# All scores of the first batch computed in the first steps, ten steps of them kept in DRAM

## The chip, the cores and the metric

The kernel runs on one core of a Trainium2 chip. A core has TensorE (PE) for matmuls, with weight loads on a lane of their own (PEld), VectorE (DVE), ScalarE (ACT), GpSimd (POOL) and SyncE (SP), which here only issues DMAs. Each engine takes its instructions in program order; they wait for each other by semaphores. The metric is the time of one execution on the device in microseconds (us), lower is better.

## What is computed

```python
def _attn_ref(q, k, v):
    B, H, S, D = q.shape                      # 8, 8, 576, 64
    scores = np.matmul(q, k.transpose(0, 1, 3, 2)) / np.sqrt(D)
    kth = np.partition(scores, -32, axis=-1)[..., -32:-31]
    scores = np.where(scores >= kth, scores, -1e9)
    scores = scores - np.max(scores, axis=-1, keepdims=True)
    attn = np.exp(scores)
    attn = attn / (np.sum(attn, axis=-1, keepdims=True) + 1e-09)
    return np.matmul(attn, v)
...
h = x @ w_in                                  # x: 4608 x 512, w_in: 512 x 2048
g = np.where(h > 0, h, np.exp(np.minimum(h, 0)) - 1)
out = g @ w_out                               # 2048 x 512
```

Attention in which every query keeps its 32 highest scores, and behind it a feed-forward block with elu. x is the attention's output with the heads side by side. The weights arrive as 64-bit floats, and the kernel decodes them to 32 bits itself.

## The kernel before

**Steps.** The attention is cut into 144 steps, 18 for each of the 8 batches. A step is one tile of 128 queries for one pair of heads (hp 0 to 3). A batch has 4 full query tiles times 4 pairs, 16 steps, and 2 steps for its last 64 queries, each of which takes two pairs at once. In batch 0 steps 0 to 3 are tile 0 with pairs 0 to 3, steps 4 to 7 tile 1, and so on; steps 16 and 17 are the remainder. A main loop runs over n, and in turn n several steps are in work: the scores of n+2 (and n+3), the search for the top 32 of step n on DVE, mask, exp, transposition and product with V of the steps before.

**Of one step.** `transpose_qk` (line 259) turns keys and queries of a pair into a tile kq of 128 x 2 x 576 numbers: PE transposes to PSUM (266, 274) and ACT copies (271, 279). `scores` (292) does a step in two halves: matmuls to a PSUM tile (309), and ACT copies it to the tile sc (329). A full step has 8 matmul records, a remainder step 20. `first_max` (331) and `next_max` (338) on DVE find the 8 highest four times over and strike them out in between (334, 340, 346): 14 instructions of 0.74 us each, which is 9.64 us a step. `biases` and `mask` on POOL (351 to 359), `exp` on ACT (367), `trans` on PE (407, 425) with two ACT copies to et (412, 426), `attend` on PE (440). When a query tile has all its pairs, `sums` (374) inverts the sums of exp by way of a small DRAM tile (382, 394) and `normalise` on POOL (455) ends a tile xT, the input of the feed-forward block.

**Feed-forward pieces** (475 to 511) are small bundles of PE work. `feed` (527) deals them out to the turns by a plan of shares and due times: it counts pieces and turns and knows no times.

**Weights.** In the steps 0 to 6 (EARLY is 6) the weights are decoded beside the attention, one at each `weight_slot` (201): ACT splits a weight into two parts (183, 184), two slots later DVE joins them (189, 190) and POOL adds (194). The slots stand between the DVE instructions of a step, four in a step up to step 3 and six from step 4 on. Raw weights lie in buffers that become free with POOL's add; SP issues the next read (173) behind that.

**Keys.** In the first steps the four pairs of batch 0 are turned on the chip, two before the loop, one each in turns 0 and 1. `keep_kq` (281) writes each kq to DRAM (283), and `load_kq` (285) brings it back for later steps (289). Steps 0 to 3 use the tile on the chip; each later step of a batch reads its pair again, a remainder step two pairs. For batch 0 that is 4 writes and 16 reads of 576 KB. The scores of steps 2 to 7 are computed in turns 0 to 5, those from step 8 on in turns 6, 8, 10 and so on, two steps at a time.

**Buffers.** kq has 5, sc 5 and two spare tiles that are raw weight buffers at first, PSUM tiles for scores and transposes (ps_x) 2. The pool xT has 2: at first they take inputs of `load_qk` (214) for the pairs (0,1) and (0,2) and later (1,1), (1,2) and (2,0), then the feed-forward inputs. SP has 8 semaphores for its DMAs and uses them in turn, so a DMA goes out only when the eighth before it has landed.

The order of each engine is the order in which the program is written (`manual_schedule`); nothing is moved by a scheduler.

Of the kernel before, what the change touches and what calls it, by code (L numbers as in the profile page):

```python
# [10 lines left out]
FP32 = mybir.dt.float32  # L11
# [24 lines left out]
class Step:  # L36
# [5 lines left out]
    def __init__(self, n, g, hp, last):  # L42
        self.n = n
        self.g = g
        self.hps = (hp, hp + 1) if g.rem else (hp,)
        self.ends = self.hps[-1] == last
        self.turned = self.attended = self.summed = False


# [12 lines left out]
def kernel(  # L62
# [9 lines left out]
    nc = tc.nc  # L72
# [7 lines left out]
    NHP = H // 2  # L80
# [47 lines left out]
    def spare_tile(i, name):  # L128

        size = ((2 * J + 2) * P, 2 * S, 2 * WN)[i // 2]  # L130
        return spare.tile([P, size], FP32, tag=f"s{i}", name=name)
# [126 lines left out]

    def transpose_qk(b, hp):

        t = kqT[b, hp] = kqpool.tile([P, 2, S], FP32, tag="kq", name="kq")
        src = [loaded.pop((b, hp, name)) for name in "kq"]
        ps = ps_x.tile([P, 2, JP], FP32, tag="x", name="qkps")
        for n in range(2):
            for c in range(J):
                nc.tensor.transpose(  # L266
                    ps[:, n, c * P : (c + 1) * P],
                    src[n][:, c, :, :].rearrange("p h d -> p (h d)"),
                    ident[:],
                )  # L270
        nc.scalar.copy(t[:, :, 0:JP], ps[:])  # L271
        ps = ps_x.tile([P, 2, JP], FP32, tag="x", name="qkps")
        for n in range(2):
            nc.tensor.transpose(
                ps[:, n, 0:R],
                src[n][0:R, J, :, :].rearrange("p h d -> p (h d)"),
                ident[0:R, 0:R],
            )
        nc.scalar.copy(t[:, :, JP:S], ps[:, :, 0:R])

    def keep_kq(b, hp):
        kept[b, hp] = dram.tile([P, 2, S], FP32, tag=f"kq{b}{hp}", name="kqd")
        nc.sync.dma_start(kept[b, hp][:], kqT[b, hp][:])
# [5 lines left out]
            nc.sync.dma_start(u.kq[hp][:], kept[u.g.b, hp][:])  # L289


    def scores(u, half):
        g = u.g
        q0 = g.qt * P
        if half == 0:
            i = (u.n + 2) % 7 if u.n >= 10 else 0
            if i < 5:
                u.sc = scpool.tile([P, 2, S], FP32, tag="sc", name="sc")
            else:
                u.sc = spare_tile(i - 3, "sc").rearrange(  # L300
                    "p (i s) -> p i s", i=2
                )
        ks = slice(half * HS, (half + 1) * HS)

        ps = ps_x.tile([P, 2, JP], FP32, tag="x", name="scps")

        def product(j, hp, i, rows, at, keys):
            r = slice(i * D, (i + 1) * D)
            nc.tensor.matmul(  # L309
                ps[rows, j, at : at + keys.stop - keys.start],  # L310
                u.kq[hp][r, 1, q0 : q0 + g.ql],
                u.kq[hp][r, 0, keys],
                start=True,
                stop=True,
            )

        if g.rem:
            for i in range(2):
                k0 = half * HS + i * R
                n = min(HS, S - k0)  # L320
                for j, hp in enumerate(u.hps):
                    product(j, hp, i, (lo, hi)[i ^ j], 0, slice(k0, k0 + n))
                if n < HS:
                    for j, hp in enumerate(u.hps):
                        product(j, hp, i, (lo, hi)[i ^ j], n, slice(0, HS - n))
        else:
            for i in range(2):
                product(i, u.hps[0], i, slice(0, P), 0, ks)
        nc.scalar.copy(u.sc[:, :, ks], ps[:, :, 0:HS])  # L329
# [258 lines left out]
    def decode(n, place):  # L588

        if place in ((3, 4, 5, 6) if n < NHP else (0, 2, 3, 4, 5, 6)):  # L590
            weight_slot()
# [3 lines left out]
    def at(step, fn, *args):  # L595
        todo.setdefault(step, []).append((fn, args))
# [5 lines left out]
    for p, pair in enumerate(pairs):  # L602
        if p >= NHP:
            n = next((n for n in extra if p in extra[n]), None)
            if n is None:
                n = EARLY + 1 + 2 * (p - 10)
                turns[n] = pair
            at(n + 1, keep_kq, *pair)
        elif p >= 2:
            at(p - 1, keep_kq, *pair)  # L610
    for n, u in enumerate(steps[NHP:]):
        at(n + 1 if n + NHP < EARLY + 2 else (n + NHP) // 2 * 2 - 3, load_kq, u)
    for hp in range(1, NHP):
        at(hp, load_v, 0, hp)
    for b in range(1, B):
# [3 lines left out]
    with tc.manual_schedule():  # L619
        for hp in range(3):  # L620
            load_qk(0, hp)
        load_weights(3)
        for hp in range(2):
            transpose_qk(0, hp)
            steps[hp].kq = {hp: kqT[0, hp]}
            for half in range(2):
                scores(steps[hp], half)
            if hp == 0:
                load_qk(0, 3)
        load_weights()  # L630
        load_v(0, 0)
        first_max(steps[0])
        weight_slot()
        weight_slot()
        for hp in range(2):
            keep_kq(0, hp)
        for n in range(NS + 4):
            early = n < EARLY
            now, last, done = (
                steps[n + d] if 0 <= n + d < NS else None for d in (0, -1, -2)  # L640
            )
            for fn, args in todo.pop(n, []):
                fn(*args)
            gone = None
            if early:
                ahead = steps[n + 2]
                if n + 2 < NHP:
                    transpose_qk(0, n + 2)
                    ahead.kq = {n + 2: kqT[0, n + 2]}
                for half in range(2):  # L650
                    scores(ahead, half)
            elif n % 2 == 0:

                for d in (2, 3):
                    if n + d < NS:
                        for half in range(2):
                            scores(steps[n + d], half)
                    if d == 2:
                        for u in steps[n - 4 : n - 2]:
                            if not u.attended:  # L660
                                attend(u)
                                gone = u
            if n in turns:
                transpose_qk(*turns[n])
            if n >= EARLY and n + 2 in turns:
                load_qk(*turns[n + 2])
            if now and n > 0:
                first_max(now)
            if last:
                biases(last)  # L670
                mask(last, 0)
            if early:
                if last:
                    mask(last, 1)
                decode(n, 0)
                feed(n, 0.5)
                if last:
                    exp(last, 0)
                    exp(last, 1)
                next_max(now, (n, 1))  # L680
                decode(n, 2)
                if last:
                    trans(last)
                feed(n, 0.5)
                next_max(now, (n, 3))
                decode(n, 4)
                if last and last.ends:
                    load_weights(margin=0)
                    sums(last)
                if last:  # L690
                    attend(last)
                next_max(now, (n, 5))
                decode(n, 6)
                if last and last.ends:
                    normalise(last.g)
                for p in extra.get(n, []):
                    transpose_qk(*pairs[p])
                for p in fetch.get(n, []):
                    load_qk(*pairs[p])
                continue  # L700
            decode(n, 0)
            feed(n, (0.3, 0.7)[n % 2])
            if now:
                next_max(now, (n, 1))
            decode(n, 2)
            if last:
                mask(last, 1)
                exp(last, 0)
            if done and not done.turned:
                trans(done)  # L710
            if now:
                next_max(now, (n, 3))
            decode(n, 4)
            if gone and gone.ends:
                normalise(gone.g)
            feed(n, (0.3, 0.7)[n % 2])
            if now:
                next_max(now, (n, 5))
            decode(n, 6)
            if last:  # L720
                exp(last, 1)
            if done and done.ends and not done.summed:
                sums(done)
        while ffn:
            ffn.pop(0)[1]()
# [33 lines left out]
```

## Time and profile before

| | |
|---|---|
| time, median of 3 runs | 1669.07 us (1668.19 to 1669.85) |
| the profiled execution | 1668.57 us, its span 1666.8 us |
| PE busy | 1574.8 us (94%) |
| PEld busy | 1049.1 us (63%) |
| DVE busy | 1461.8 us (88%) |
| ACT busy | 918.2 us (55%) |
| POOL busy | 1154.1 us (69%) |
| granted PE clock, mean | 0.970 |
| DMA | 176.86 MB, mean 106 GB/s |

The profile is of one execution. A row of a timeline gives start, length, engine, line, operation, the tile written and the tiles read, their shapes, and in brackets the engine's idle time before and what ended it. A row of waits gives the total, the times and the longest. A busy share is a mean over stages of different kind: the first 136 us hold seven steps with weight decoding, then steps follow each other at 9.6 to 10.2 us, and after step 143 (1521 us) only feed-forward work is left. Matmul ends are modelled, so a busy PE is not PE at its peak.

### The profile page before, as it was taken

How to read it: one execution, taken by the hardware profiler on the slowest of the kernel's cores; microseconds unless marked ns; L12 is line 12 of the kernel's file. 1: busy time of each engine (PE TensorE's matmuls, PEld its weight loads, DVE VectorE, ACT ScalarE, POOL GpSimd, SP SyncE). 2: the span in 40 equal slices, each digit the busy share in tenths (PEclk: the TensorE clock that was granted, in tenths of full speed). 3: DMA queues.
4: the chain of work that ended last, by engine and by line, in shares of the span. 5: the costliest groups of instructions: out<-in, count | busy, mean ns of one | idle time of the engine just before them, and what ended most of it. 6: DMA issues, size and time to landing. Idle time of an engine off the chain costs nothing.

```text
span 1666.8 us, 28300 instructions
## 1 busy us (share of the span) xinstructions
PE 1574.8 (94%) x9792; PEld 1049.1 (63%) x9792; DVE 1461.8 (88%) x3065; ACT 918.2 (55%) x1877; POOL 1154.1 (69%) x1462
## 2 busy tenths in 40 slices
PE   5559899999999999998999999999999999999999
PEld 3346777777776675857566566566556566566565
DVE  6989999999999999999999989979989989987000
ACT  5566566566656564646466466456466466355121
POOL 4777777777778786878778678668668668668021
PEclk7569999999999999999999999999999999999999
DMA  9873555445363513121212321221212312210000
GB/s 329 227 242 124 162 163 147 148 145 154 111 198 96 190 39 117 64 84 70 85 71 100 112 88 61 77 84 64 91 70 100 112 60 89 77 42 8 26 7 13
DMA packets 139552, 176.86 MB, mean 106 GB/s; under 512 B 94352, under 2 KB 102544, under 8 KB 139408
## 3 DMA queue, kind: packets, MB, share of 16 engines
q1 hardware_dynamic: 135856, 174.16, 32.5%
q8 instruction: 78, 1.28, 0.3%
q10 hardware_dynamic: 3552, 0.89, 0.3%
q14 instruction: 66, 0.54, 0.1%
HBM read 146.54 MB, written 28.46 MB: 105 GB/s over the span
## 4 chain that ended last, share of the span: by engine, by line
PE 61%; DVE 24%; POOL 5%; issue 4%; ACT 4%; DMA 2%; SPq 1%; ACTq 0%; POOLq 0%; DVEq 0%
PE ops L499 21%; PE hps L475 20%; DVE m L346 11%; DVE wk L340 10%; PE scps L309 7%; PE avps L440 6%; PE eps L407 5%; DVE m L334 2%; POOL sc L359 1%; PE qkps L266 1%; POOL wk L357 1%; POOL wk L358 1%; POOL gT L492 1%; ACT sc L367 1%; DMA qin<-in_q_dram 1%
## 5 line engine op out<-in xcount | busy, mean ns | idle before, releaser
L346 DVE MAX8 m<-wk 128x8 f32<-128x576 f32 x864 | 609.5, 747 | 0.0
L475 PE MATMUL hps<-xT,w_in 128*128 128x128 f32 (+2 forms) x2432 | 531.7, 373 | 10.9 <-ACT gT L490 5.7
L499 PE MATMUL ops<-w_out,gT 128*128 128x512 f32 x1152 | 520.0, 597 | 7.1 <-ACT osb L508 7.1
L475 PEld LDWEIGHTS hps<-xT,w_in 128*128 128x128 f32 x2432 | 381.5, 192 | 136.1 <-issue 18.8
L359 POOL TENSOR_TENSOR sc<-sc,wk 128x576 f32<-128x576 f32 x288 | 407.1, 1414 | 23.9
L340 DVE MATCH_REPLACE8 wk<-m,wk 128x576 f32<-128x576 f32 x576 | 423.4, 743 | 0.0
L499 PEld LDWEIGHTS ops<-w_out,gT 128*128 128x128 f32 x1152 | 209.6, 190 | 240.3 <-issue 214.3
L367 ACT ACTIVATE sc<-sc,neg 128x576 f32<-128x576 f32 x288 | 224.1, 778 | 226.5 <-POOL sc L359 226.3
L492 POOL TENSOR_TENSOR gT<-gT,n 128x384 f32<-128x384 f32 (+1 forms) x168 | 187.3, 1121 | 192.3 <-ACT n L491 189.4
L357 POOL TENSOR_SCALAR wk<-sc,nth 128x576 f32<-128x576 f32 x288 | 215.5, 748 | 28.0
L329 ACT COPY sc<-scps 128x576 f32<-128x576 f32 x288 | 170.2, 639 | 89.9 <-PE scps L309 87.7
L309 PE MATMUL scps<-kq 64*128 64x288 f32 (+3 forms) x1344 | 187.7, 430 | 29.8 <-ACT kq L271 17.8
L340 DVE MATCH_REPLACE8 wk<-m,sc 128x576 f32<-128x576 f32 x288 | 211.7, 743 | 0.0
L334 DVE MAX8 m<-sc 128x8 f32<-128x576 f32 x288 | 201.2, 740 | 11.1 <-ACT sc L329 11.0
L358 POOL TENSOR_SCALAR wk<-wk 128x576 f32<-128x576 f32 x288 | 192.2, 667 | 23.8
L412 ACT COPY et<-eps 128x1024 f32<-128x1024 f32 x144 | 144.6, 1004 | 98.3 <-PE eps L407 97.3
L440 PE MATMUL avps<-et,vE 128*64 128x128 f32 (+1 forms) x3200 | 180.2, 269 | 6.1 <-ACT et L412 3.8
L440 PEld LDWEIGHTS avps<-et,vE 128*64 128x64 f32 x3200 | 162.0, 139 | 33.8 <-issue 25.1
L407 PEld LDWEIGHTS eps<-ident,sc 128*128 128x128 f32 x1152 | 135.7, 143 | 72.8 <-issue 36.6
L407 PE MATMUL eps<-ident,sc 128*128 128x128 f32 x1152 | 154.6, 277 | 21.8 <-ACT sc L367 19.7
L309 PEld LDWEIGHTS scps<-kq 64*128 64x128 f32 (+1 forms) x1344 | 104.9, 180 | 101.2 <-issue 39.5
L489 ACT ACTIVATE n<-hps 128x384 f32<-128x384 f32 (+1 forms) x168 | 90.1, 536 | 115.7 <-PE hps L475 107.3
(60 smaller groups left out, 910.0 us busy)
## 6 DMA issues: line engine op xcount, KB each, us to landing
kq<-kqd SPq DMA_DIRECT2D x156, 576.0 KB
kqd<-kq SPq DMA_DIRECT2D x32, 576.0 KB
rb<-recd SPq DMA_DIRECT2D x64, 128.0 KB
out_dram<-osb SPq DMA_DIRECT2D x32, 256.0 KB
kin<-in_k_dram SPq DMA_DIRECT2D x27, 256.0 KB
qin<-in_q_dram SPq DMA_DIRECT2D x26, 256.0 KB
raw<-in_moe_w_out_dram SPq DMA_DIRECT2D x12, 512.0 KB
vE<-in_v_dram SPq DMA_DIRECT2D x32, 128.0 KB
```

Of the source, the lines that this page charges most:

```text
L309: nc.tensor.matmul(ps[rows, j, at : at + keys.stop - keys.start], u.kq[hp][r, 1, q0 : q0 + g.ql], u.kq[hp][r, 0, keys], start=True, stop=True,
L334: nc.vector.max(u.m1[:, i, :], u.sc[:, i, :])
L340: nc.vector.match_replace(u.wk[:, i, :], u.m[:, i, :], u.cur[:, i, :], TAKEN)
L346: nc.vector.max(u.m[:, i, :], u.cur[:, i, :])
L357: nc.gpsimd.tensor_scalar(pen, s, u.nth[:, i : i + 1], 2.0**100, ALU.add, ALU.mult)
L358: nc.gpsimd.tensor_scalar(pen, pen, 0.0, TAKEN, ALU.min, ALU.max)
L359: nc.gpsimd.tensor_tensor(s, s, pen, ALU.add)
L367: nc.scalar.activation(s, s, AF.Exp, bias=u.neg[:, i : i + 1], scale=scale, accum_out=g.den[:, at : at + 1],)
L407: nc.tensor.transpose(ps[:, i, c * P : (c + 1) * P], e[:, k0 + c * P : k0 + (c + 1) * P], ident[:],)
L440: nc.tensor.matmul(g.av[r, hp, 0:ql], vE[g.b, hp][:, i, (c + i) % (J + 1), :], u.et[:, at, q0 : q0 + ql], start=(c == 0), stop=(c == J),)
L475: nc.tensor.matmul(ps[:, f % G, :], w_in[:, i, f * P : (f + 1) * P], blk.xT[:, i, 0:N], start=(i == 0), stop=(i == NC - 1),)
L499: nc.tensor.matmul(blk.o[:], blk.gT[f // NG][:, f % NG, s * P : (s + 1) * P], w_out[:, f, :], start=(f == 0), stop=(f == NF - 1),)
```

## The change

In batch 0 the keys are no longer written to DRAM and read back. The scores of all 18 steps are computed in turns 0 to 4 from the kq tiles on the chip (the line with `g.b > 0` in the diff). Those of steps 2 to 7 go directly to their sc tiles, as before, except that steps 6 and 7 are both done in turn 4. Those of steps 8 to 17 go through `scores_ahead`: ACT copies them to a tile of the pool xT (two buffers), SP writes this to DRAM, and `load_scores` reads it to the sc tile in turns 6, 8, 10, 12 and 14, where the scores were computed before. Where in a turn: steps 8, 9 at the end of turn 0; 10, 11 in turn 1 ahead of the exps, 12, 13 at its end; 14, 15 and 16, 17 the same in turn 2. A write is issued behind the next score of its kind or at the end of the turn. DVE's and POOL's instructions and their order are the same before and after; so are the feed-forward pieces.

```diff
+    def score_tile(u):
+        i = (u.n + 2) % 7 if u.n >= 10 else 0
+        if i < 5:
+            u.sc = scpool.tile([P, 2, S], FP32, tag="sc", name="sc")
+        else:
+            u.sc = spare_tile(i - 3, "sc").rearrange("p (i s) -> p i s", i=2)
+
+    waiting = []
+
+    def store_scores():
+        while waiting:
+            u, t = waiting.pop(0)
+            nc.sync.dma_start(u.scd[:], t)
+
+    def scores_ahead(u):
+        t = xtpool.tile([P, NC, T], FP32, tag="xT", name="scin")
+        t = t[:].rearrange("p c n -> p (c n)")[:, 0 : 2 * S]
+        u.sc = t.rearrange("p (i s) -> p i s", i=2)
+        for half in range(2):
+            scores(u, half)
+        u.scd = dram.tile([P, 2, S], FP32, tag=f"sc{u.n}", name="scd")
+        store_scores()
+        waiting.append((u, u.sc))
+        u.sc = None
+
+    def load_scores(u):
+        score_tile(u)
+        nc.sync.dma_start(u.sc[:], u.scd[:])
+
     def scores(u, half):
...
+        if u.sc is None:
+            score_tile(u)
+        kq = u.kq if g.b > 0 else {hp: kqT[0, hp] for hp in u.hps}
...
-        elif p >= 2:
-            at(p - 1, keep_kq, *pair)
-    for n, u in enumerate(steps[NHP:]):
-        at(n + 1 if n + NHP < EARLY + 2 else (n + NHP) // 2 * 2 - 3, load_kq, u)
+    direct = {n: (n + 2,) for n in range(EARLY - 2)}
+    direct[EARLY - 2] = (EARLY, EARLY + 1)
+    ahead = {(0, 1): (8, 9)}
+    for n in (1, 2):
+        ahead[n, 0] = (4 * n + 6, 4 * n + 7)
+        ahead[n, 1] = (4 * n + 8, 4 * n + 9)
+    for u in steps[first[1] :]:
+        at(u.n // 2 * 2 - 3, load_kq, u)
...
-        for hp in range(2):
-            keep_kq(0, hp)
...
             if early:
-                ahead = steps[n + 2]
                 if n + 2 < NHP:
                     transpose_qk(0, n + 2)
-                    ahead.kq = {n + 2: kqT[0, n + 2]}
-                for half in range(2):
-                    scores(ahead, half)
+                for m in direct.get(n, ()):
+                    for half in range(2):
+                        scores(steps[m], half)
             elif n % 2 == 0:
                 for d in (2, 3):
-                    if n + d < NS:
+                    if n + d < first[1]:
+                        load_scores(steps[n + d])
+                    elif n + d < NS:
                         for half in range(2):
                             scores(steps[n + d], half)
...
                 if last:
                     mask(last, 1)
+                for m in ahead.get((n, 0), ()):
+                    scores_ahead(steps[m])
                 decode(n, 0)
                 feed(n, 0.5)
                 if last:
...
                 decode(n, 6)
+                for m in ahead.get((n, 1), ()):
+                    scores_ahead(steps[m])
+                store_scores()
```

More of the change, by code (lines that the diff above doesn't have):

```diff
@@ L46, in __init__ @@
         self.ends = self.hps[-1] == last
+        self.sc = self.scd = None
         self.turned = self.attended = self.summed = False
@@ L294, in scores @@
         q0 = g.qt * P
[L295 to L302, printed above, removed]
+        if u.sc is None:
+            score_tile(u)
+        kq = u.kq if g.b > 0 else {hp: kqT[0, hp] for hp in u.hps}
         ks = slice(half * HS, (half + 1) * HS)
@@ L310, in product @@
                 ps[rows, j, at : at + keys.stop - keys.start],
-                u.kq[hp][r, 1, q0 : q0 + g.ql],
-                u.kq[hp][r, 0, keys],
+                kq[hp][r, 1, q0 : q0 + g.ql],
+                kq[hp][r, 0, keys],
                 start=True,
@@ L624 @@
             transpose_qk(0, hp)
-            steps[hp].kq = {hp: kqT[0, hp]}
             for half in range(2):
```

## The prediction, made before the changed kernel was run

> **What bounds the kernel now.** I read the busy shares first, then the DVE's waits, then the timelines of DVE, ACT and SP step by step. A step n runs from its first max (line 334) to that of step n+1; steps 1 to 7 start at 25.88, 41.94, 58.07, 74.19, 93.98, 118.50 and 136.26 us on the DVE timeline, step 18 at 246.87. The page calls PE busy 94% of the span and names it on 61% of the chain, which invites the thought that 12 us taken off PE are 12 us gained. The windows by stage speak against it (columns: stretch, length, then PE, PEld, DVE, ACT, POOL busy with counts, granted PE clock, DMA share, GB/s):
>
> ```profile
> 25.88:41.94 16.06, 7.68 (x37) 5.09 (x37) 15.59 (x30) 9.74 (x19) 12.05 (x14) 0.50 1.03 401
> 41.94:58.07 16.13, 8.89 (x45) 6.02 (x45) 15.58 (x29) 8.60 (x17) 12.06 (x14) 0.52 0.98 309
> 136.26:246.87 110.61, 103.44 (x820) 78.85 (x820) 108.48 (x231) 64.43 (x129) 81.13 (x105) 0.97 0.48 147
> ```
>
> In steps 1 and 2 DVE works 15.6 of 16.1 us while PE works half of the time; from step 7 to 17 DVE works 108.48 of 110.61. Through all of the first batch DVE sets the pace, and a change can gain there only what DVE idles. These are its waits of the first 250 us, start and trifles aside (us in total, times, longest):
>
> ```profile
> DVE w_out L189 <- ACT w_out L183: 7.8, 4, 2.5
> DVE wk L340 <- POOL sc L359: 1.9, 1, 1.9
> ...
> DVE w_in L189 <- ACT w_in L183: 1.4, 4, 0.4
> ```
>
> 9.2 us are waits for ACT's weight split (line 183), in steps 0 to 6; 1.9 us is a wait for POOL in step 12. So **ACT's in-order queue is the thing to watch**: DVE's join of a weight stands a slot or two behind ACT's split of it, with hardly any slack. Step 1 on ACT shows how the queue runs:
>
> ```profile
> 28.66 0.64 ACT L329 COPY sc<-scps 128x576 f32<-128x576 f32 x1 [1.27 <-PE scps L309]
> 29.62 0.64 ACT L329 COPY sc<-scps 128x576 f32<-128x576 f32 x1 [0.32 <-PE scps L309]
> 31.21 0.78 ACT L367 ACTIVATE sc<-sc,neg 128x576 f32<-128x576 f32 x1 [0.94 <-POOL sc L359]
> ...
> 34.65 0.78 ACT L367 ACTIVATE sc<-sc,neg 128x576 f32<-128x576 f32 x1 [2.58 <-POOL sc L359]
> ...
> 36.72 1.01 ACT L412 COPY et<-eps 128x1024 f32<-128x1024 f32 x1 [1.21 <-PE eps L407]
> ...
> 37.79 0.67 ACT L183 ACTIVATE w_in<-w_out 128x512 f32<-128x512 f32 x1
> ```
>
> and DVE waits for that last split:
>
> ```profile
> 38.49 0.43 DVE L189 TENSOR_SCALAR w_in<-w_in 128x512 uint32<-128x512 uint32 x1 [0.33 <-ACT w_in L183]
> ```
>
> What the change puts between 29.62 and 31.21 on ACT shows on DVE, as soon as it is longer than the wait for POOL.
>
> **Part 1, the new wait in step 1: +9.7 us.** The ten scores that go by way of DRAM are copied by ACT into the pool of two xT buffers. The third (step 10) takes the buffer of the first (step 8) and so waits until the DRAM write of that has landed. When is that? In the built order the writes of scores 8 and 9 stand on SP exactly where the first two key writes stood, same form (128x1152), same count of DMAs ahead:
>
> ```profile
> 33.80 0.47 SPq L256 DMA_DIRECT2D vE<-in_v_dram  x1
> 35.13 2.93 SPq L283 DMA_DIRECT2D kqd<-kq  x3
> 40.11 0.32 SPq L289 DMA_DIRECT2D kq<-kqd  x1
> ```
>
> The first key write goes out at 35.13 and the read of it, which must wait for its landing, at 40.11. The trace's landing marks give 40.05 and, for the second, 41.43. Nothing earlier is to be had: SP had been held by earlier reads (1.5 MB weights) to 33.8.
>
> Now ACT in the new order: splits of step 0 end at 26.24; copies of scores 8 and 9; key copies of head pair 3; copies of score 3; copies of scores 10, 11; exp. PE and ACT alternate on two PSUM buffers, at about 0.96 us a half (28.66 to 29.62). That brings score 3's copies to about 35.7, where ACT stands still until 40.1. Copies of 10: 40.1 to 41.3. PE refills one half after the first copy; copies of 11: 41.9 to 43.4. The two exps: 43.4 to 45.2, the second from 44.3 instead of 34.65. That is 9.65 later; transposes, et copy and the split behind it follow as before (34.65 to 37.79 is 3.14), so the split starts at 47.4, and DVE's join goes out at 48.1 instead of 38.49. Behind the waiting copy on ACT are the exps, the et copies and four splits; PE's transposes and DVE wait for them. No cover: DVE already waits 0.33 there. Bounds: with the quickest write of this shape (80.95 to 84.70, 3.75 us) it is +8.5, with the slowest of the neighbours (44.94 to 51.69, 6.75) +11.5. I take 9.7, the same place in the queue.
>
> The Trainium skill ("DMA: Bandwidth & Descriptors", section "Anatomy of one DMA") says that a DMA costs about 2.0 us fixed, most of it the receipt for the last byte and worst when the target is HBM, plus bytes over 436 GB/s. For 589,824 bytes that is 3.35 us, an estimate by that page; by it this term would be 8.1. The row (4.92) is in a busy queue and decides.
>
> **Part 2, the same in step 2: +1.9.** Scores 12 and 13 are copied after step 1's splits (which end at 42.3 + 9.65 = 52.0), 13 until about 55.2; the writes of 12 and 13 go out at 53.2 and 55.2 and land at about 58 and 60, with 4.9 us each. Score 4's copies end at 56.9, those of 14 and 15 then run from 58.1 to 61.4. Before, the second exp of this step stood at 50.70, shifted 60.35; now it stands at 62.3: +1.9. With writes of 3.75 us it is about 0, with 6.75 it is 3.8. In exchange, the wait of PE for the key read (4.77 at 46.02) goes; it cost DVE nothing, as exp was waiting for POOL.
>
> **Part 3, step 3: 0.** Scores 16 and 17 are copied at the end of step 2, those of 5 at its start; the second exp stood at 66.84, and shifted there are 2 us of room. But the reads of key pairs 5 and 6 need the same two buffers, so they now wait for the writes of 16 and 17. Before they landed at 65.4 at the latest and were turned from 75.64 on. I get the writes landing at about 78.5, reads until about 86, needed at 77.83 + 11.6 = 89.4 by the last of them: 3 us of cover are left of 12. Bounds 0 to +5.
>
> **Part 4, step 4: +1.9.** Score 7 moves from step 5 into step 4, before the split at 83.77, for which DVE waits 2.46 (84.48). Two more halves at 0.96 us. Bounds 0 to 2.3 (PE's 2.29 for eight).
>
> **Part 5, step 5: -2.8.** The copies of score 7 go (99.76 to 101.25), and two key reads leave SP ahead of a weight read: that went out at 101.19, behind reads at 98.89 and 99.86. It lands at 108.17, in the queue behind those two, which by the landing marks take 1.5 us each; ACT and then DVE wait for it:
>
> ```profile
> 108.88 0.43 DVE L189 TENSOR_SCALAR w_out<-w_out 128x512 uint32<-128x512 uint32 x1 [2.46 <-ACT w_out L183]
> ```
>
> Landing about 2.9 earlier takes the 2.46 away and about 0.3 of the 1.1 behind it. What is late next is POOL's add, which frees the buffers. Bounds 0 to -3.6.
>
> **Part 6, steps 6 to 17: -2.2.** Ten steps' scores leave PE and ACT: 1.24 us a step on PE (8 matmuls), 12.3 in all, 11.7 on ACT. In step 6 four copies (125.07 to 128.64) stood in front of a split for which DVE waited 1.93 us (129.35): that goes. In step 12 DVE waits 1.92 for POOL's mask, which is behind the elu work; no score matmul stands before that on PE since 174.24, so I count 0.3. Everything else is beside a DVE that has no idle time: worth nothing. Bounds 0 to -3.9.
>
> **Part 7, the reads back: 0.** Ten reads of 576 KB replace 16 key reads and the 10 writes come where 4 key writes were: 20 transfers before and after. Each is issued two steps ahead (19 us); such a read takes 5 to 7 us. The first pair stands behind step 5's weight reads on SP and has 27 us. Bounds 0 to +1.
>
> **Sum:** 9.7 + 1.9 + 0 + 1.9 - 2.8 - 2.2 + 0 = **+8.5 us**, on the profiled execution's 1668.57 (span 1666.8, 1.8 around it): **1677.1**. That execution is 0.5 below the median of the three runs, so nothing is corrected. After step 17 the planner deals the same pieces in the same order, DVE idles less than 0.1 us a step until step 81, and the shift passes to the end.
>
> **Rivals.**
> 1. PE is the bound, as its 94% says: -12.3 us, 1656. Against it: DVE's 9.64 us a step without a gap. Chance 0.03.
> 2. Faster, on the other side: the writes land before ACT reaches copy 10, at about 35.7 instead of 40.05, in step 1, and at 56.9 instead of 58 in step 2. Then parts 1 and 2 are near 0 (the second exp waits for POOL until 34.65 anyway), and 1.9 - 2.8 - 2.2 = -3.1 to -7 (bounds of 5 and 6) remain: about 1664. That takes a write of under 1 us, and no row of this size is under 3.75, or a write that goes out before 31, and SP is held to 33.8. Chance 0.10.
> 3. Worse: the writes take as long as the slowest neighbour (6.75 to 7.2), in all of the five pairs. Then +11.5 + 3.8, and pairs 5 and 6 of the keys come 3 to 5 us too late for PE at the end of step 3, which reaches DVE by way of the copies in front of the split at 83.77. About +17, 1686. Chance 0.17.
> 4. The waits are there, but smaller (6 us), and parts 5 and 6 give all that DVE idled: within 3.3 us of now. Chance 0.12.
>
> **How the numbers follow.** My forecast has 0.58. Range 1667 to 1690: all of it, rival 3 with the upper bounds of parts 1 to 4 (11.5 + 3.8 + 5 + 2.3, less about 2), and most of rival 4; left out are rivals 1 and 2 and a little of 4. About 0.2% (3.3 us) is what a measurement can tell from no change: faster 0.13, same 0.12, slower 0.75.
>
> **What would show it.** Right: ACT's third score copy into the DRAM buffers ends a wait for a DMA at about 40, the second exp stands near 44, DVE's wait for ACT's split in step 1 is 8 to 11 us, step 1 lasts about 25.7; DVE waits near 108.9 and 129 (shifted) gone; from step 7 the same 9.64 a step. Wrong: no wait of ACT for a DMA in step 1, or DVE's idle time in steps 7 to 17 grows (score reads late), or steps there get shorter than 9.6.

## The result, and the profile after

The changed kernel takes 1680.88 us (median of 4 runs, 1679.46 to 1683.83); the kernel before, run beside it, 1669.46 (median of 4, 1668.19 to 1670.47). The ratio is 1.0071, with a 95% interval of 1.0054 to 1.0089: 0.7% slower. The profiled execution is the longest of the four (1683.83 us, span 1682.0), 3 us above the median; where that matters below, it is said.

Lines have moved: the weight split is now 184 and 185, the join 190 and 191, the score copy 356, the score matmuls 336, exp 394, the et copy 439, the mask 386. New are 306 (write of a score to DRAM) and 322 (its read). Steps 1, 2, 3, 6 and 18 of DVE start at 26.93, 53.04, 69.66, 129.61 and 258.60 us. The windows of step 1, step 2 and steps 7 to 17:

```profile
26.93:53.04 26.11, 15.14 (x79) 10.10 (x79) 15.58 (x29) 14.38 (x27) 12.04 (x14) 0.64 0.86 313
53.04:69.66 16.62, 12.99 (x85) 7.45 (x81) 15.60 (x30) 13.37 (x25) 12.08 (x14) 0.74 0.68 224
...
149.09:258.60 109.51, 94.92 (x692) 72.99 (x692) 108.08 (x231) 53.58 (x110) 78.58 (x103) 0.93 0.47 146
```

Read them by columns against those of before. Step 1 has the same 15.58 us of DVE work but lasts 26.11 us instead of 16.06. In steps 7 to 17 PE is relieved of 8.5 us (103.44 to 94.92) and ACT of 10.9 (64.43 to 53.58), and the stage gets only 1.1 us shorter (110.61 to 109.51): DVE's 108 us were the length of it. DVE's waits up to 265 us, start and trifles aside:

```profile
DVE w_in L190 <- ACT w_in L184: 12.7, 5, 10.4
...
DVE w_out L190 <- ACT w_out L184: 10.6, 4, 4.3
DVE wk L367 <- POOL sc L386: 1.2, 1, 1.2
```

Before, the two waits for ACT's split were 1.4 and 7.8, together 9.2; now they are 23.3, and one of them alone is 10.4. ACT in step 1 shows it being made:

```profile
33.60 1.18 ACT L356 COPY sc<-scps 128x576 f32<-128x576 f32 x2 [0.69 <-PE scps L336]
41.32 1.18 ACT L356 COPY scin<-scps 128x576 f32<-128x576 f32 x2 [6.54 <-DMA scd<-scin]
43.44 0.64 ACT L356 COPY scin<-scps 128x576 f32<-128x576 f32 x1 [0.93 <-PE scps L336]
...
45.66 0.76 ACT L394 ACTIVATE sc<-sc,neg 128x576 f32<-128x576 f32 x1
...
48.88 0.68 ACT L184 ACTIVATE w_in<-w_out 128x512 f32<-128x512 f32 x1
```

Score 3 is copied at 33.60; then ACT stands still for 6.54 us, until the DRAM write of score 8 has landed (41.22 by the landing marks) and its buffer may take score 10. Behind that copy the second exp is at 45.66 (34.65 before) and the split at 48.88 (37.79 before). DVE pays for it at once:

```profile
49.60 0.43 DVE L190 TENSOR_SCALAR w_in<-w_in 128x512 uint32<-128x512 uint32 x1 [10.39 <-ACT w_in L184]
```

DVE's later waits, in steps 4, 5, 6 and 12:

```profile
97.77 0.43 DVE L190 TENSOR_SCALAR w_out<-w_out 128x512 uint32<-128x512 uint32 x1 [4.17 <-ACT w_out L184]
119.58 1.28 DVE L190 TENSOR_SCALAR w_out<-w_out 128x512 uint32<-128x512 uint32 x1 [1.44 <-ACT w_out L184]
...
145.14 0.43 DVE L190 TENSOR_SCALAR w_out<-w_out 128x512 uint32<-128x512 uint32 x1 [4.34 <-ACT w_out L184]
200.45 0.09 DVE L367 MATCH_VALUE_LOAD wk<-m,sc 128x8 f32 x1 [1.22 <-POOL sc L386]
```

Before, DVE's only wait in step 6 was this one, behind four score copies on ACT:

```profile
129.35 1.33 DVE L189 TENSOR_SCALAR w_out<-w_out 128x512 uint32<-128x512 uint32 x1 [1.93 <-ACT w_out L183]
```

The one at 145.14 is new in kind. Its split on ACT waited 8.95 us for the weight to arrive:

```profile
144.45 0.66 ACT L184 ACTIVATE w_out<-raw 128x512 f32<-128x512 f32 x1 [8.95 <-DMA raw<-in_moe_w_out_dram]
```

SP's own rows (start, length of the issue, line, what is moved, how many), before and then after:

```profile
123.82 0.33 SPq L283 DMA_DIRECT2D kqd<-kq  x1
124.25 0.38 SPq L173 DMA_DIRECT2D raw<-in_moe_w_out_dram  x1
124.68 2.93 SPq L289 DMA_DIRECT2D kq<-kqd  x2
```

```profile
134.78 1.55 SPq L322 DMA_DIRECT2D sc<-scd  x2
136.43 0.41 SPq L174 DMA_DIRECT2D raw<-in_moe_w_out_dram  x1
```

The two score reads of turn 6 (576 KB each) stand directly ahead of the last weight read. Before, the two key reads stood behind it. By the landing marks the weight took 8.0 us from issue to landing, before 6.0.

The whole account, from the steps of DVE in the two profiled executions (us; "term" is what the prediction gave):

| step | before | after | difference | term |
|---|---|---|---|---|
| 0 | 14.04 | 15.04 | +1.0 | none |
| 1 | 16.06 | 26.11 | +10.05 | +9.7 |
| 2 | 16.13 | 16.62 | +0.5 | +1.9 |
| 3 | 16.12 | 16.13 | 0.0 | 0 |
| 4 | 19.80 | 21.01 | +1.2 | +1.9 |
| 5 | 24.52 | 22.81 | -1.7 | -2.8 |
| 6 | 17.76 | 19.49 | +1.7 | -1.9 |
| 12, 13 | 22.79 | 21.24 | -1.55 | -0.3 |
| 17, 23, 33 | 30.04 | 33.30 | +3.3 | 0 |

All other steps together make +0.7; the sum is 15.2, the distance of the two spans. Steps 17, 23 and 33 together are 3.3 us of it; other kernels do not have these (see e4 and e5).

### The profile page after: what moved, and what is told of

Same layout as the page of the kernel before. It is cut to its first block, busy times and chain, and to the rows that moved or that the text cites. A ratio compares the mean times of both kernels' runs of the same rounds, so it can differ in the third digit from the quotient of the medians.

```text
span 1682.0 us, 28316 instructions
## 1 busy us (share of the span) xinstructions
PE 1584.5 (94%) x9792; PEld 1055.2 (63%) x9792; DVE 1461.0 (87%) x3065; ACT 918.8 (55%) x1877; POOL 1155.0 (69%) x1462
## 4 chain that ended last, share of the span: by engine, by line
PE 60%; DVE 21%; POOL 6%; issue 4%; ACT 4%; DMA 3%; SPq 1%; POOLq 0%; ACTq 0%; DVEq 0%
PE ops L526 21%; PE hps L502 20%; DVE m L373 9%; DVE wk L367 9%; PE scps L336 7%; PE avps L467 6%; PE eps L434 5%; POOL sc L386 2%; DVE m L361 2%; POOL wk L384 1%; POOL gT L519 1%; POOL wk L385 1%; DMA raw<-in_moe_w_out_dram 1%; ACT sc L394 1%; DMA raw<-in_moe_w_in_dram 1%
## 5 line engine op out<-in xcount | busy, mean ns | idle before, releaser
L502 PE MATMUL hps<-xT,w_in 128*128 128x128 f32 (+2 forms) x2432 | 535.7, 375 | 18.2 <-ACT gT L517 11.3
L502 PEld LDWEIGHTS hps<-xT,w_in 128*128 128x128 f32 x2432 | 385.4, 194 | 141.9 <-issue 17.1
L336 PE MATMUL scps<-kq 64*128 64x288 f32 (+3 forms) x1344 | 191.3, 436 | 26.3 <-ACT scin L356 12.2
L356 ACT COPY sc<-scps 128x576 f32<-128x576 f32 x268 | 158.3, 640 | 81.3 <-PE scps L336 79.3
L467 PEld LDWEIGHTS avps<-et,vE 128*64 128x64 f32 x3200 | 162.9, 140 | 32.0 <-issue 25.3
```

What stands on the lines that cost most here:

```text
L336: nc.tensor.matmul(ps[rows, j, at : at + keys.stop - keys.start], kq[hp][r, 1, q0 : q0 + g.ql], kq[hp][r, 0, keys], start=True, stop=True,)
L467: nc.tensor.matmul(g.av[r, hp, 0:ql], vE[g.b, hp][:, i, (c + i) % (J + 1), :], u.et[:, at, q0 : q0 + ql], start=(c == 0), stop=(c == J),)
L502: nc.tensor.matmul(ps[:, f % G, :], w_in[:, i, f * P : (f + 1) * P], blk.xT[:, i, 0:N], start=(i == 0), stop=(i == NC - 1),)
```

## The experiments

Theory A: ACT's order in the first turns makes the loss. Whatever stands ahead of a weight split is paid by DVE: the wait for the two buffers, the copies themselves, and, on SP, whatever stands ahead of a weight read. Rivals: that score work in the first steps is too much wherever it stands; that the score reads lack bandwidth; that late differences are the phase of PE's clock. The before-kernel run beside e1 to e5 took 1668.52 us (median), beside e6 to e8 1668.99, beside e9 to e11 1668.62. Step lengths are of each kernel's one profiled execution.

| kernel | median us | ratio to before, 95% | steps 1 to 3 | step 4 | step 5 | step 6 |
|---|---|---|---|---|---|---|
| before | 1669.46 | 1 | 48.3 | 19.8 | 24.5 | 17.8 |
| after | 1680.88 | 1.0071 (1.0054 to 1.0089) | 58.9 | 21.0 | 22.8 | 19.5 |
| e1 five buffers | 1673.52 | 1.0032 (1.0019 to 1.0045) | 50.9 | 22.2 | 25.0 | 19.1 |
| e2 end of turn | 1677.05 | 1.0051 (1.0037 to 1.0064) | 53.9 | 22.2 | 23.5 | 19.5 |
| e4 reads late | 1679.63 | 1.0066 (1.0054 to 1.0079) | 58.8 | 21.0 | 25.0 | 16.0 |
| e5 keys first | 1678.67 | 1.0062 (1.0049 to 1.0074) | 60.4 | 20.1 | 21.7 | 18.9 |
| e6 score 7 late | 1678.35 | 1.0051 (1.0038 to 1.0063) | 59.2 | 20.2 | 25.0 | 18.4 |
| e7 four scores | 1667.80 | 0.9989 (0.9980 to 0.9998) | 48.3 | 19.8 | 25.3 | 16.0 |
| e8 five edits | 1667.95 | 0.9992 (0.9983 to 1.0001) | 48.1 | 19.7 | 26.3 | 17.3 |
| e9 e8, late writes | 1668.78 | 0.9999 (0.9990 to 1.0008) | 48.9 | 19.8 | 22.7 | 17.7 |
| e10 e7, late writes | 1667.79 | 0.9996 (0.9987 to 1.0005) | 47.9 | 19.8 | 22.9 | 18.2 |
| e11 before, late writes | 1670.45 | 1.0012 (1.0003 to 1.0021) | 48.3 | 19.8 | 25.8 | 18.2 |

After, e4 and e5 are the same program up to turn 6. Their step 1 lasted 26.11, 26.24 and 27.94 us, their step 5 22.81, 24.97 and 21.72: one execution tells a step of this stage to about 2 us, and a row must be seen before a smaller difference is believed. Two of these spreads have a row. Steps 0 and 1 together take 41.15, 41.33 and 41.51 us (30.10 before): the write lands at 41.2 to 41.6 us in all three and fixes their end, and a longer step 0 only makes step 1 shorter. And step 5 goes with POOL's wait for the sums' round trip through DRAM: in the ten kernels with scores ahead of time it takes 21.7 to 23.5 us where POOL waits at most 1.2 us for it, and 25.0 to 26.3 where POOL waits 1.9 to 3.8.

### Five buffers (e1)

```diff
-        t = xtpool.tile([P, NC, T], FP32, tag="xT", name="scin")
-        t = t[:].rearrange("p c n -> p (c n)")[:, 0 : 2 * S]
+        home = {10: 0, 11: 1, 14: 2, 15: 0}.get(u.n)
+        if home is None:
+            t = xtpool.tile([P, NC, T], FP32, tag="xT", name="scin")
+            t = t[:].rearrange("p c n -> p (c n)")[:, 0 : 2 * S]
+        else:
+            t = w_out[:].rearrange("p f d -> p (f d)")
+            t = t[:, home * 2 * S : (home + 1) * 2 * S]
```

Expected: 

> Scores 10, 11, 14, 15 are copied to a part of w_out that is free in turns 1 and 2, instead of the two xT buffers, so that no copy has to wait for a DRAM write. Theory A (ACT stands still in step 1 because copy 10 needs the buffer whose DRAM write lands at 41.2): the wait of 6.54 us on ACT goes, copies 10 and 11 end near 38.4 behind score 3's, the second exp stands near 39.3 instead of 45.66, step 1 lasts about 19.7 us instead of 26.1, step 2 is unchanged, and the time is about 6 us below the changed kernel: 1675. Rival B (what costs is the added work of PE and ACT itself, and the DRAM wait only lies beside it): step 1 stays above 24, the time at 1680. Rival C (all of it is the wait): step 1 is back at 16.1 to 17, time 1671.

Measured: 1673.52 us. ACT waits for no score write any more, and step 1 lasts 18.88 us. ACT and then DVE in step 1:

```profile
35.74 1.24 ACT L361 COPY w_out<-scps 128x576 f32<-128x576 f32 x2 [0.31 <-PE scps L341]
...
37.64 0.76 ACT L399 ACTIVATE sc<-sc,neg 128x576 f32<-128x576 f32 x1
...
40.31 0.71 ACT L184 ACTIVATE w_in<-w_out 128x512 f32<-128x512 f32 x1
```

```profile
41.05 0.43 DVE L190 TENSOR_SCALAR w_in<-w_in 128x512 uint32<-128x512 uint32 x1 [3.12 <-ACT w_in L184]
```

So of the 10.05 us that step 1 gained, about 7.2 were the wait for a buffer (26.11 less 18.88), and about 2.8 (18.88 less 16.06) are the four copies of scores 10 and 11 themselves, which now stand without any wait between POOL's mask and the exps. By steps 0 and 1 together (41.15, 32.51 and 30.10 us) it is 8.6 and 2.4. That is a second price, and taking the wait away does not take it away.

### Score work only at the ends of turns, two buffers (e2)

```diff
-        ahead[n, 0] = (4 * n + 6, 4 * n + 7)
-        ahead[n, 1] = (4 * n + 8, 4 * n + 9)
+        ahead[n, 1] = tuple(range(4 * n + 6, 4 * n + 10))
```

Expected: 

> The two xT buffers stay; scores 10, 11 and 14, 15 move from ahead of the exps to the end of their turns, in front of 12, 13 and 16, 17. Theory A: nothing stands before the exps of step 1 but the copies of 8, 9 and 3: step 1 about 17.3; the wait comes back between 11 and 12 and between 15 and 16, in front of the exps of steps 2 and 3, but writes take only some 3 us there: step 2 about 18.5 instead of 16.6, step 3 about 18.0 instead of 16.1. Sum about -5: 1676. Rival B (the added work of ACT and PE costs, wherever it stands): steps 1 to 3 together as long as in the changed kernel (58.9 us), time 1680 to 1681.

Measured: 1677.05 us. The wait for the buffers is still there, in four smaller pieces; ACT's waits up to 120 us:

```profile
ACT scin L356 <- DMA scd<-scin: 5.7, 4, 1.8
```

Steps 1 to 3 are 15.62, 19.98 and 18.32 us. The loss moved from step 1 to steps 2 and 3 and halved (53.9 us in the three, 58.9 after, 48.3 before). Neither the place alone nor the buffers alone removes it.

### Score reads behind the weight reads (e4)

```diff
-                        load_scores(steps[n + d])
+                        pass
...
+            if n % 2 == 0 and n + 2 < first[1]:
+                for d in (2, 3):
+                    load_scores(steps[n + d])
```

The second part stands at the end of a turn.

Expected: 

> Only the reads of the stored scores move, from the start of turns 6, 8, 10, 12, 14 to their ends, in turn 6 so behind the last weight read. Theory A (step 6 lost 1.7 us since two score reads of 576 KB now stand on SP in front of the last weight read, for which ACT waits 8.95 us and DVE 4.34): the weight read lands some 3 us earlier, DVE's last wait in step 6 falls from 4.3 to about 1.5, step 6 from 19.5 to about 16.7, time 1678. Rival (the weight read is late since POOL's add frees its buffer late): step 6 stays at 19 to 19.5 and the time at 1680 to 1681. If reads that late miss their steps, DVE waits for them at the starts of steps 8, 10, ...: then the time is above 1681.

Measured: 1679.63 us, which its interval does not tell from after. The profile does: SP's order in turn 6 is turned round,

```profile
136.94 0.38 SPq L174 DMA_DIRECT2D raw<-in_moe_w_out_dram  x1
137.37 1.38 SPq L322 DMA_DIRECT2D sc<-scd  x2
```

and DVE has no wait left in step 6, which lasts 16.04 us, all of it work (19.49 with 4.48 idle after). The weight read goes out no earlier than in after (136.94 against 136.43), so its buffer is not what was late; it lands 5.0 us after its issue instead of 8.0. The cause of that stall is shown: the place on SP. Steps 17, 23 and 33 were at their old length too (10.19, 9.64, 10.20). The time shows it less, since step 5 was 2.2 us longer in this execution: POOL waits 2.0 us for the sums there, and not at all in after. In e1 and e6, whose step 5 was as long, step 6 with the reads in front still took 19.1 and 18.4 us.

### Key reads of steps 18 and 19 ahead of the last score reads (e5)

After spends 3.1 us of PE's time waiting for these keys:

```profile
237.27 0.67 PE L336 MATMUL scps<-kq 64*64 64x288 f32 x2 [2.40 <-DMA kq<-kqd]
238.62 1.60 PE L336 MATMUL scps<-kq 64*64 64x288 f32 x18 [0.68 <-DMA kq<-kqd]
```

```diff
-        at(u.n // 2 * 2 - 3, load_kq, u)
+        at(14 if u.n < 20 else u.n // 2 * 2 - 3, load_kq, u)
```

Expected: 

> Only the key reads of steps 18 and 19 (four, 576 KB each) move from turn 15 to turn 14, so that SP issues them before the score reads of steps 16 and 17. Theory A (PE waits 3.1 us for these keys at 237 because two score reads now stand before them; PE has no slack after that, elu and POOL's masks come later, and DVE's waits grow by 2 us in step 23 and 0.4 to 0.8 in steps 17 and 33): PE's wait for kq falls under 0.5, steps 17, 23 and 33 are back at 10.2, 9.7 and 10.2, the time 1677 to 1678. Rival (these differences are of that one execution, whose time was the longest of four): steps 23 and 33 differ anyhow, time 1680 to 1681.

Measured: 1678.67 us. PE's wait is gone and steps 17, 23 and 33 are at their old length. But the score read of step 16 now stands behind, and DVE stalls there:

```profile
236.70 1.42 DVE L361 MAX8 m<-sc 128x8 f32<-128x576 f32 x2 [1.33 <-POOL wk L384]
```

POOL's line 384 in the bracket belongs to another step; what this max reads is the tile of step 16, whose read went out at 231.06, behind four key reads, and landed at 236.61 by the landing marks. One stall of 3 us was traded for one of 1.3. The size of the first is not fixed: e2 had 2.3 us of it and 0.9 us in steps 17 and 33, e1, e4 and e6 (0.5, 0.2 and 0.3) had none there.

### Score 7 at the end of turn 4 (e6)

```diff
-    direct[EARLY - 2] = (EARLY, EARLY + 1)
+    direct[EARLY - 2] = (EARLY,)
...
+                if n == EARLY - 2:
+                    for half in range(2):
+                        scores(steps[EARLY + 1], half)
```

Expected: 

> The changed kernel with one edit: score 7 is computed at the end of turn 4, behind the weight splits of that turn, instead of in its middle. Theory A (what stands ahead of a weight split on ACT is paid by DVE, copy by copy): the two halves of score 7, 2 x 0.6 to 0.96 us, leave the place ahead of the split in step 4, so step 4 falls from 21.0 to about 19.8 us and the stall of DVE there from 4.2 to about 2.7 to 3.0; the copies now stand ahead of the first split of step 5, where up to 1 us comes back. Time 0 to 1.2 us below the changed kernel, about 1680. Rival B (the extra 1.2 us of step 4 is the phase of PE's clock and not the copies): step 4 stays at 20.8 to 22.2.

Measured: 1678.35 us. Step 4 took 20.17 us instead of 21.01 and its stall 3.34 instead of 4.17, two thirds of what was expected. But e5, in which score 7 stands where it stands in after, had a step 4 of 20.11 us, so this difference cannot be put down to the copies. Step 5 was 24.96, which lies within the spread of after's program. Inconclusive: rival B, PE's clock, stays open, and how much of step 4's loss the copies make is not shown.

### Four scores ahead of time only (e7)

On the kernel before: scores 8 and 9 at the end of turn 1, 10 and 11 at the end of turn 2, copied to a free part of w_out, read back at the ends of turns 6 and 8. Keys are written as before, and read for all other steps.

```diff
+    ahead = {1: (8, 9), 2: (10, 11)}
+    early_steps = [m for ms in ahead.values() for m in ms]
...
+        if u.n in early_steps:
+            continue
...
+                for m in ahead.get(n, ()):
+                    scores_ahead(steps[m])
...
+            for d in (2, 3):
+                if n % 2 == 0 and n + d in early_steps:
+                    load_scores(steps[n + d])
```

Expected: 

> The kernel before with only the part that gained: scores 8 and 9 at the end of turn 1 and 10 and 11 at the end of turn 2, copied to a free part of w_out, written to DRAM and read back at the end of turns 6 and 8; all other scores and the keys stay as in the kernel before, except that no key is read for these four steps. Theory A (the loss of the change is the place of its copies on ACT and the two buffers; its gain is step 5's and step 6's stall): steps 1 to 3 within 1 us each of before, step 5 about 22 instead of 24.5 (two key reads are off SP ahead of a weight read), step 6 about 16 instead of 17.8 (no score copies ahead of the split): 3 to 5 us below the kernel before, 1664 to 1666. Rival B (any score work in turns 1 and 2 costs DVE its own length): four scores are 8 copies, about 5 to 6 us in steps 2 and 3, which eats the gain: within 2 us of before.

Measured: 1667.80 us, 0.11% below before (0.02 to 0.20%), less than theory A's 3 to 5 us. Its first half holds to the tenth: steps 1 to 3 take 16.06, 16.11 and 16.11 us, so eight copies at the ends of two turns cost nothing there (rival B had 5 to 6 us; its time, within 2 us of before, came for another reason), and step 6 is 16.04 without a stall. The gain hoped for in step 5 didn't come (25.26 instead of 22): POOL waits there.

```profile
99.10 2.00 POOL L476 TENSOR_TENSOR xT<-xT,rb 128x512 f32<-128x512 f32 x1 [3.73 <-DMA rb<-recd]
```

### Five edits at once (e8)

e1, e2, e4, e5 and e6 together.

Expected: 

> The changed kernel with five edits at once: five buffers instead of two for the ten scores, score work only at the ends of turns, score 7 at the end of turn 4, score reads behind the weight reads, key reads of steps 18 and 19 early. Theory A (the loss is these five places and nothing else): the terms of the single runs add up, -8 for buffers and turn ends together (the two overlap: 58.9 us in steps 1 to 3 falls to about 50), -3 for the late score reads, -1 for the stalls of steps 17 to 33: 1668 to 1672, level with the kernel before. Rival B (20 copies on ACT and 12 us of PE at half clock are too much for the first three steps wherever they stand): steps 1 to 3 still 52 to 54 us and the time 1674 to 1677.

Measured: 1667.95 us, ratio 0.9992: level with the kernel before. The windows of steps 1 and 2:

```profile
26.89:42.51 15.62, 9.60 (x57) 6.74 (x59) 15.50 (x29) 11.97 (x23) 12.07 (x14) 0.74 0.98 376
42.51:58.84 16.33, 13.39 (x77) 7.57 (x77) 15.60 (x30) 13.60 (x25) 12.06 (x14) 0.83 0.82 293
```

Same scores, same DRAM traffic, same work as after, and DVE idles 0.1 us in step 1 instead of 10.5. The rival of too much work for the first steps is out: the 11 us were the places and the two buffers. What e8 also shows is what remains when the loss is repaired. All scores ahead of time gain nothing, because DVE's steps 7 to 17 were full already: they take 109.1 us in e8, 107.6 of them DVE's work, and took 110.6 before.

### Key writes at the ends of turns 4 and 5 (e9, e10, e11)

Step 5 stayed at 25 to 26 us in e7 and e8. In both, POOL's normalisation waits 3.7 to 3.8 us for the round trip of the sums through DRAM; POOL's masks follow, then the second exp, then a weight split for which DVE waits. On SP three key writes and a weight read go out just ahead of the sums, and by the landing marks the four small writes of the sums (1 KB each) then take 4.3 to 4.9 us.

```diff
-            at(n + 1, keep_kq, *pair)
+            if 4 <= p <= 8:
+                late.setdefault(n + 1, []).append(pair)
+            else:
+                at(n + 1, keep_kq, *pair)
...
                 decode(n, 6)
+                for pair in late.get(n, ()):
+                    keep_kq(*pair)
```

Expected of e8 with this: 

> The kernel with all five edits, and besides it the key writes of the five pairs turned in turns 3 and 4 (three in turn 4, two in turn 5) go from the start of the turn to its end, behind the weight reads and the round trip of the sums. In the kernel with five edits POOL waits 3.8 us in step 5 for that round trip (rb), because SP sends it behind three key writes and a weight read that lands at 94.2; the masks, the second exp (108.80) and the weight split behind it (109.57) follow late, and DVE waits 4.5. Theory C (step 5's stall is the place of DMAs ahead of the sums' round trip): the weight read lands about 3 to 4 us earlier, the second exp comes 2 to 3 us earlier, idle of DVE in step 5 falls from 6.7 to about 3 to 4, time 1664 to 1666. Rival D (the stall is the weight read itself, or POOL's add that frees its buffer): step 5 stays at 25 to 26 us, time as before.

Expected of e7 with this: 

> The kernel before with four scores ahead, and the same five key writes moved to the end of their turns. There POOL waits 3.7 us for the round trip in step 5, and the second exp stands at 108.07. Theory C: idle of DVE in step 5 from 5.4 to about 2 to 3, time about 1665. Rival D: step 5 at 25 us, time 1668.

Expected of before with this: 

> The kernel before with the same five key writes moved to the end of their turns, nothing else. There the round trip comes in time (POOL waits 0.46), and DVE waits 2.5 for a weight read that stands on SP behind two key writes and two key reads. With the two writes gone from ahead of it, that read lands about 2 us earlier: step 5 from 24.5 to about 23 us, time 0 to 2 us below the kernel before. Since the two key reads stay ahead, not more than that. The writes may now delay the reads of inputs behind them: up to 1 us the other way.

Measured: POOL's normalisation in e8,

```profile
99.97 1.90 POOL L487 TENSOR_TENSOR xT<-xT,rb 128x512 f32<-128x512 f32 x1 [3.83 <-DMA rb<-recd]
```

and in e9:

```profile
97.77 1.27 POOL L487 TENSOR_TENSOR xT<-xT,rb 128x512 f32<-128x512 f32 x1 [1.05 <-issue]
```

The second exp of step 5 on ACT in e8,

```profile
108.80 0.78 ACT L399 ACTIVATE sc<-sc,neg 128x576 f32<-128x576 f32 x1 [2.20 <-POOL sc L391]
```

and in e9:

```profile
106.83 0.78 ACT L399 ACTIVATE sc<-sc,neg 128x576 f32<-128x576 f32 x1 [2.49 <-POOL sc L391]
```

The small writes of the sums land after 1.2 us in e9 and in e10. POOL's idle time ahead of the normalisation went from 3.83 to 1.05 us and the exp came 2 us earlier; step 5 fell from 26.25 to 22.67 in e9 and from 25.26 to 22.91 in e10, as theory C says.

The time did not follow: 1668.78 against 1667.95, and 1667.79 against 1667.80, where rival D had put it and not the 1664 to 1666 of theory C. In step 6 two of the key writes now stand on SP between the other weight reads and the last one, which goes out no earlier than without the edit (126.61 against 125.97 in e9, 125.17 against 124.37 in e10), and DVE idles 2.6 and 3.2 us there instead of 0.2 and 0. In e10 step 6 takes back 2.2 of the 2.35 us. In e9 it takes back only 0.3 of 3.6, since DVE's own work in step 6 was 2.1 us shorter (15.04 instead of 17.14); its step 1 was 1.8 us longer (17.40 instead of 15.62). Why e9's median did not fall is not shown. In the kernel before, where the round trip came in time, the edit only costs (e11: 0.12%, step 5 25.83 where 23 was expected).

## Why the prediction was right, and where it was wrong

The forecast of 1677.1 us, 0.5% slower, stands against 1680.88, 0.7% slower: the sign and the main mechanism were right, the size 3 us short. The parts' errors cancel in the sum to some extent: parts 1, 5 and 6 came out dearer than forecast, part 2 and steps 12 and 13 cheaper.

- **What bounds the kernel.** Right. PE lost 8.5 us in steps 7 to 17 and the stage 1.1.
- **Part 1** (+9.7). Right in mechanism: ACT's wait for a DMA ended at 41.32 ("about 40"), the second exp stood at 45.66 ("near 44"), DVE's wait was 10.4 ("8 to 11"). The landing took 5.9 us from issue (35.36 to 41.22 by the landing marks), between the 4.9 taken and the 6.75 of the upper bound. That step 1 shows +10.05 all the same is luck: step 0 was 1.0 us longer in this execution, and step 1 shorter by it. Steps 0 and 1 together gained 11.05 us, and 11.2 to 11.4 in e4, e5 and e6, so the term was 1.4 to 1.7 us too small, 0.9 of it by the longer landing. The estimate worked out from the Trainium skill's "DMA: Bandwidth & Descriptors", section "Anatomy of one DMA", was 3.35 us; that section gives its fit for DMAs issued by GpSimd, and these go out from SP. Rows of this trace lie on both sides of it: this write took 5.9 us, and the writes of scores 12 and 13 (issued at 54.58 and 57.07, nothing between 45.02 and the first of them) landed after 2.8 and 3.1 us.
- **Part 2** (+1.9, measured +0.5). Mis-sized by just those two writes, which were taken as 4.9. The "quickest write of this shape" of 3.75 us, which bounded parts 1 and 2 and, as "no row of this size is under 3.75", rival 2, was not the quickest of the trace before: several key writes from 270.94 us on landed after 3.4 to 3.7.
- **Part 3** (0) and **part 4** (+1.9, measured +1.2 in after and +0.3 in e5, the same program so far) held within their bounds. What the copies make of part 4 is not shown (e6).
- **Part 5** (-2.8, measured -1.7). The weight read did land earlier, by 3.1 us counted from the start of step 5 (2.9 in the forecast), but "what is late next is POOL's add" was wrong: next in after is POOL's second mask, for which the second exp waits 3.67 us (118.11). Where the sums' round trip is late too, the masks hang on that: in e4 POOL waits 2.0 us for it and step 5 is 0.45 us longer than before, not shorter.
- **Part 6**, the step that failed: "In step 6 four copies (125.07 to 128.64) stood in front of a split for which DVE waited 1.93 us (129.35): that goes." The copies went, and the wait became 4.34 us. Part 7 had put the score reads at 0, asking what they wait behind and how much cover they have ("27 us"), and not who waits behind them. They stand on SP ahead of the last weight read; e4 moved them and the step took 16.04 us, 1.7 less than before, which is the -1.9 of the forecast but for 0.2. That is 3.7 us in this step; the medians differ by 11.4 us where 8.5 were forecast, 2.9 more.
- **Part 7** (0, bounds to +1) also missed the keys of steps 18 and 19, which stand behind the score reads of 16 and 17: up to 3.3 us in steps 17 to 33, in some executions. Against this, steps 12 and 13 gave 1.55 instead of 0.3.
- **Rivals.** Rival 1 (PE is the bound) is refuted. Rival 2 named the right condition and a wrong price: without the wait for the buffers, parts 1 and 2 are not "near 0". e1 has no wait and step 1 still lasts 2.8 us longer. The reason given, that the exp waits for POOL until 34.65 anyway, left out that four copies end only at about 37. Rival 2's lower end is a slip of its sum, too: 1.9 with the bounds of parts 5 and 6 (-3.6 and -3.9) is -5.6 and not -7. Rival 3's total (+17) did not come; its landing time was met halfway in step 1 (5.9 of 6.75 us, 4.9 taken), and passed by one write alone (7.6 us, issued at 62.18).

Not settled: what the copies of score 7 cost in step 4 (e6), why e9's median did not follow its step 5, and why one of the four small writes of the sums landed after 2.9 us in e4 and after 1.2 in after, in the same order of issues, which is what made POOL wait in e4.

## What to carry to other kernels

Moving work off an engine that the busy shares call full gained nothing here, since another engine's own work filled the stage; compare the stage's length with each engine's busy time in it first. When a step is moved, list for every in-order queue it enters (ACT, SP) what stands behind it and who waits for that: here four such places and the two buffers were worth all of the 11 us (e8), and the work itself nothing. A buffer that is freed by a DRAM write is a wait for that write's landing, in the order of the engine that fills it. And when one program's executions differ in a step, look at the sum with its neighbours before a term is called right.

## What the runs showed of the hardware that was not expected

PE's granted clock changed several times within a step. Eight score matmuls in after, at four places:

```profile
27.99 2.29 PE L336 MATMUL scps<-kq 64*128 64x288 f32 x8 [3.69 <-ACT scin L356]
...
32.80 1.24 PE L336 MATMUL scps<-kq 64*128 64x288 f32 x8 [0.84 <-ACT kq L273]
...
42.01 2.29 PE L336 MATMUL scps<-kq 64*128 64x288 f32 x8 [6.43 <-ACT scin L356]
...
51.28 2.29 PE L336 MATMUL scps<-kq 64*128 64x288 f32 x8
```

The granted clock over these rows is 0.50, 1.00, 0.50 and 0.50. Behind a gap of 3.69 us they take 2.29 us, 4 us later 1.24, and behind a gap of 6.43 again 2.29. The Trainium skill ("TensorE: Matmul & The Clock Gate", section "Part 1: The HAM clock gate") names an idle window of about 3.4 us after which the clock falls to half. The first three rows fit that; the fourth, with no gap ahead of it, is as slow, so the gap just ahead does not tell the clock by itself. More PE work went with a higher clock here: the granted clock of step 2 rose from 0.52 before (8.9 us of PE work) to 0.74 in after (13.0) and 0.83 in e8 (13.4).

The 1.0 us of step 0 goes with this clock in all twelve profiled executions. In after, e4, e8 and e9 the first stretch of full clock that the trace records begins at 17.3 to 17.6 us, and step 0 lasts 14.8 to 15.1; in the other eight kernels it begins at 11.9 to 13.6, and step 0 lasts 13.6 to 14.1. The same eight matmuls of step 0 take 2.29 us in after (at 14.17) and 1.24 in e5 (at 14.22), and up to there the two are one program.

A DRAM write of one and the same shape landed between 2.8 and 7.6 us after its issue in one execution (54.58 and 62.18). Ahead of the first SP had issued nothing since 45.02, ahead of the second a weight read of 512 KB at 61.48.
